# A two-branch linear-attention kernel on one core: x and V of the first two tiles by blocks of 128 rows, the first fold half a V later, the sums of K of tile 15 behind Q 12

## The chip, the core and the metric

The kernel runs on one core of a Trainium2 chip. A core has a matrix engine (TensorE, "PE" in the profile, with a separate row "PEld" for its weight loads), VectorE ("DVE"), ScalarE ("ACT"), GpSimd ("POOL") and SyncE ("SP"), which here issues nearly all DMAs. Each engine executes its own list of instructions in the order in which the program wrote it; semaphores hold an instruction back until what it reads has been written. The metric is device time in microseconds (us) of one execution, the median over runs.

## The reference

Two branches A and B of the same form read the same x and differ in weights only. S is 2048, D is 448, there are 16 heads of 28.

```python
qkv = (x @ wqkv).reshape(B, S, 3, H, Dh)            # q, k, v per head
pq  = einsum("bhsd,hdf->bhsf", q, w_phi)            # pk the same from k
phi_q = concat([softmax(pq), softmax(-pq)])         # over the 28 features; phi_k too
kv  = einsum("bhsf,bhsd->bhfd", phi_k, v);  z = phi_k.sum(s)
num = einsum("bhqf,bhfd->bhqd", phi_q, kv)
o   = num / (einsum("bhqf,bhf->bhq", phi_q, z) + 1e-6)
out_branch = o.reshape(B, S, D) @ wo
g   = sigmoid((x * gate_w).sum(-1))
result = g * out_A + (1 - g) * out_B
```

No position waits for an earlier one, but the sum kv over all 2048 positions has to be complete before the first num.

## The kernel before

The 2048 positions go in 16 tiles of 128. f32 accuracy comes from splitting each operand in a high part (written by ACT) and a low part (the rest, by a subtraction on DVE or POOL); one projection of a tile in one branch is 11 matmuls (4 high by high, 4 high by low, 3 low by high; the last 64 rows of x carry their low part in the same block). w_phi is multiplied into the weights of K and Q once, at the start: this is the fold. There are four folds F 0 to F 3, each one group of matmuls into the bank F, one transpose on DVE out of the bank (L363, into `ret` for F 0 and F 2, into `ru` for F 1 and F 3), high parts on ACT (`rk` for K, `rq` for Q) and low parts on DVE or POOL.

The stages, in the order of PE's program: 22 short warm-up records of matmuls on zeros (11 matmuls, L640, and 12 small ones, L643); V of tiles 0 and 1 (`v_first`, L448), in which the first block of x, the raw weights of V and their split arrive piece by piece; V of tiles 2 to 4 with the four folds between them; then for each tile K, Q and V projections (L416), the accumulation of kv (L501, name `T`), and at the end num (`N`, L583) and the output projection (`O`, L631) by pairs of tiles.

What follows K of a tile t (`k_soft`): ACT copies it to `pk`; DVE takes its maximum and minimum per head (`mx`, L482 and L483); POOL subtracts (`ret<-pk,mx` and `ret<-mx,pk`); ACT takes exp; DVE sums (`sm`, L489) and takes the reciprocal (L490); POOL multiplies (`ret<-ret,sm`). The two halves are called e. kv of two tiles needs their four multiplied halves. What follows Q (`q_front`, `q_soft`): DVE takes `qmx` (L516) out of the bank Q and writes `ru<-Q,qmx` twice, which frees the bank; four DMAs write that to `qd`, one reads it back; minimum `qmn` (L535), subtraction on POOL, exp, sums `qsm` (L541), multiplication and a transpose on DVE (L546). Of early tiles the result is spilled to DRAM and fetched back before num.

wo is rearranged in DRAM (`wos`, a row of copies from `in_wo`), and `split_wo` takes its seven blocks one after the other: load into `wst`, high part on ACT, low part on POOL (`wst<-wst`), and two stores to `wod`. One buffer serves all seven.

Who does what in which order is decided by the class `Plan`. Each step is added with engine, cost, latency and what it reads and writes; PE's steps stand in the order of the generator `steps()`. `order()` then simulates all engines and gives each free engine the ready step with the earliest due time; an extra `ahead` or `now` moves a step's due time, and a step with `two` set holds POOL and DVE apart from each other in that simulation. The result is a fixed list per engine. So a change in one place can move steps of another engine far away, because their turn is found anew.

```python
def split_wo(c):
    add("SP", 0.4, dma(s[0], wos[:, :, c]...), [...("wos", c)...], [("ws", 0)], lat=2.4, kb=229)
    put("ACT", D, act(f[1], s[0]), [("ws", 0)], [("ws", 1)])
    put("POOL", D, tt("POOL", f[2], s[0], s[1], OP.subtract), [("ws", 0), ("ws", 1)], [("ws", 2)])
```

## Time and profile before

| | before |
|---|---|
| median of 3 runs | 338.69 us (338.41 to 338.84) |
| the profiled execution | 338.63 us |
| its span in the trace | 336.8 us |
| PE busy | 330.2 us, 98% |
| DVE busy | 280.1 us, 83% |
| POOL busy | 251.0 us, 75% |
| ACT busy | 144.7 us, 43% |

The span runs from the first to the last instruction that the trace shows; 1.83 us of the profiled execution lie around it. A busy PE here means that PE had a matmul in flight: matmuls are pipelined, so their durations overlap, and the distance between the starts of two of them is what one costs. A row of the timeline gives start, duration, engine, line, operation, output and inputs, the count of merged neighbours, and in brackets how long the engine had been idle and what ended that. A weight load or matmul that starts late shows PE's waits; everything on the other engines counts only as far as it makes PE start late.

### The profile page before, as it was taken

To read this page: it belongs to the slowest core of one execution; us is meant where nothing else is said; L and a number is where in the kernel's file an instruction comes from. 1 tells how busy PE (TensorE), PEld (TensorE's weight loads), DVE (VectorE), ACT (ScalarE), POOL (GpSimd) and SP (SyncE) were. 2 spreads that over 40 slices of the span, in tenths; PEclk is the share of its full clock that TensorE was granted. 3 is DMA by queue.
4 is the path that set the end of the run, shared out by engine and by line. 5 is a ranking of instruction groups with operands and counts; after the bars stand their busy time and mean duration, and the time that the engine had idled before them with its cause. 6 is when DMAs were issued, how large, how long until landed. Compare 5 with 4: busy or idle time off the path is not lost.

```text
span 336.8 us, 8893 instructions
## 1 busy us (share of the span) xinstructions
PE 330.2 (98%) x3742; PEld 296.1 (88%) x3742; DVE 280.1 (83%) x339; ACT 144.7 (43%) x236; POOL 251.0 (75%) x210
## 2 busy tenths in 40 slices
PE   8999999999999999999999999989999999999995
PEld 7977899998999999999999999979788898788894
DVE  4547979798798795969999989985899999999960
ACT  4647845453264462624436244531052432533231
POOL 7118769999999879989896999982279768887400
PEclk9999999999999999999999999999999999999999
DMA  7882046532296847646556230875975455141011
GB/s 245 250 239 72 0 142 193 154 109 56 86 331 234 260 158 245 171 172 211 200 171 229 72 110 8 279 262 132 336 260 167 150 168 199 68 163 57 31 55 55
DMA packets 29855, 54.73 MB, mean 163 GB/s; under 512 B 4616, under 2 KB 25464, under 8 KB 27512
## 3 DMA queue, kind: packets, MB, share of 16 engines
q1 hardware_dynamic: 29560, 54.06, 49.5%
q8 instruction: 29, 0.48, 0.6%
q0 software_dynamic: 256, 0.12, 0.1%
q14 instruction: 10, 0.08, 0.1%
HBM read 31.54 MB, written 24.22 MB: 166 GB/s over the span
## 4 chain that ended last, share of the span: by engine, by line
DVE 33%; PE 30%; POOL 13%; DMA 12%; issue 5%; ACT 2%; SPq 2%; POOLq 0%; DVEq 0%; ACTq 0%
PE O L631 10%; POOL ret L263 8%; PE Q L416 5%; DMA qd<-ru 4%; DVE ret L546 4%; DVE sm L489 4%; DMA ru<-qd 4%; PE VB L416 3%; DVE qsm L541 3%; DVE ru L263 3%; DMA ed<-ret 3%; POOL rv L603 3%; DVE qmx L516 3%; PE VA L416 3%; DVE mx L482 3%
## 5 line engine op out<-in xcount | busy, mean ns | idle before, releaser
L416 PE MATMUL Q<-rq,rx 128*128 128x432 f32 x352 | 72.2, 359 | 1.3 <-DVE ru L263 1.2
L416 PE MATMUL K<-rk,rx 128*128 128x432 f32 x352 | 71.8, 359 | 0.0
L631 PE MATMUL O<-rk,rx 128*128 128x448 f32 x336 | 70.6, 368 | 0.1
L416 PEld LDWEIGHTS Q<-rq,rx 128*128 128x128 f32 x352 | 65.8, 188 | 5.4 <-DVE ru L263 2.0
L631 PEld LDWEIGHTS O<-rk,rx 128*128 128x128 f32 x336 | 62.5, 188 | 8.5 <-ACT rx L622 1.2
L416 PEld LDWEIGHTS K<-rk,rx 128*128 128x128 f32 x352 | 66.1, 188 | 3.1
L266 ACT ACTIVATE ret<-ret 128x896 f32<-128x896 f32 x48 | 45.6, 950 | 51.0 <-POOL ret L263 50.9
L263 POOL TENSOR_TENSOR ret<-ret,sm 128x896 f32<-128x896 f32 x32 | 54.0, 1707 | 3.4 <-DVE sm L490 3.3
L489 DVE TENSOR_REDUCE sm<-ret 128x32 f32<-128x896 f32 x32 | 33.7, 1070 | 4.7 <-ACT ret L266 4.7
L546 DVE STREAM_TRANSPOSE ret<-ret 128x2048 f32<-128x2048 f32 x16 | 36.5, 2283 | 1.1 <-POOL ret L263 0.8
L416 PE MATMUL VA<-rv,rx 128*128 128x450 f32 x154 | 34.3, 370 | 0.0
L541 DVE TENSOR_REDUCE qsm<-ret 128x32 f32<-128x896 f32 x32 | 33.2, 1056 | 1.3 <-ACT ret L266 1.1
L263 POOL TENSOR_TENSOR ret<-pk,mx 128x896 f32<-128x896 f32 x16 | 27.3, 1705 | 9.3 <-DVE mx L482 8.5
L416 PE MATMUL VB<-rv,rx 128*128 128x448 f32 x154 | 33.9, 367 | 0.0
L263 POOL TENSOR_TENSOR ret<-qmn,ru 128x896 f32<-128x896 f32 x16 | 28.2, 1764 | 7.1 <-DVE ret L546 4.2
L266 ACT ACTIVATE ret<-ru 128x896 f32<-128x896 f32 x16 | 15.2, 952 | 40.0 <-issue 17.4
L416 PEld LDWEIGHTS VB<-rv,rx 128*128 128x128 f32 x154 | 28.6, 188 | 3.4 <-issue 0.8
L416 PEld LDWEIGHTS VA<-rv,rx 128*128 128x128 f32 x154 | 28.7, 189 | 2.9 <-ACT rk L266 0.4
L263 POOL TENSOR_TENSOR ret<-ret,qsm 128x896 f32<-128x896 f32 x16 | 27.3, 1707 | 0.9
L263 POOL TENSOR_TENSOR ret<-mx,pk 128x896 f32<-128x896 f32 x16 | 27.3, 1706 | 0.7 <-DVE mx L483 0.7
L535 DVE TENSOR_REDUCE qmn<-ru 128x32 f32<-128x896 f32 x16 | 17.0, 1063 | 10.4 <-DMA ru<-qd 10.4
L603 POOL TENSOR_TENSOR rv<-rv,rd 128x896 f32<-128x896 f32 x14 | 23.8, 1703 | 1.1
(92 smaller groups left out, 444.3 us busy)
## 6 DMA issues: line engine op xcount, KB each, us to landing
ed<-ret SPq DMA_DIRECT2D x8, 1024.0 KB
ret<-ed SPq DMA_DIRECT2D x8, 1024.0 KB
qd<-ru SPq DMA_DIRECT2D x64, 112.0 KB
ru<-qd SPq DMA_DIRECT2D x16, 448.0 KB
out<-ret SPq DMA_DIRECT2D x16, 224.0 KB
wod<-wst SPq DMA_DIRECT2D x14, 224.0 KB
rk<-wod SPq DMA_DIRECT2D x2, 1568.0 KB
xraw<-in_xt SPq DMA_DIRECT2D x6, 512.0 KB
```

The lines of the kernel that those rows point to most:

```text
L263: return lambda: ENG[eng].tensor_tensor(val(o), val(a), val(b), op)
L266: return lambda: A.activation(val(o), val(i), f, **k)
L416: nc.tensor.matmul(bank[name][:, k, lo:hi], x[:, xc, o:o + P], w[l][:, c], start=i == 0, stop=i == len(XT) - 1)
L482: put("DVE", 2 * D, lambda: V.tensor_reduce(mh[0], pkh, AX.X, OP.max), kp, [km[0]])
L489: put("DVE", 2 * D, lambda s=s, e3=e3: V.tensor_reduce(sm[:, s], e3, AX.X, OP.add), [ke[s]], [("sm", t % 2, s)])
L516: put("DVE", 2 * D, lambda: V.tensor_reduce(mx, p4(), AX.X, OP.max), ["Q"], [km])
L535: put("DVE", 2 * D, lambda: V.tensor_reduce(qmn, tq.rearrange("p c b g f -> p c (b g) f"), AX.X, OP.min), [kt], [kn])
L541: put("DVE", 2 * D, lambda s=s, e3=e3: V.tensor_reduce(qsm[:, s], e3, AX.X, OP.add), [ke[s]], [("qsm", i, s)])
L546: add("DVE", 2.25, lambda: V.transpose(eTf[slot], eq.rearrange("p s a c f -> p (s a c f)")), ke, turned(slot))
L603: put(eng, 2 * D, lambda: ENG[eng].tensor_tensor(mid["o", n % 3].rearrange("p (c a f) -> p a c f", c=4, a=8), ctv()[:, :, i, :, :DH], rd[: ...
L631: nc.tensor.matmul(bank[pb][:, 0, :D], a, w, start=i == 0, stop=i == len(terms) - 1)
```

## The change

1. **Start.** x of tiles 0 and 1 is loaded in four DMAs of 128 rows (before: one of 128 rows and one of 384), alternating with the four loads of the raw weights of V for branch A. Its split goes by blocks: four ACT copies and four subtractions on DVE, and the one DVE copy of 384 rows (L297) is gone. V of tiles 0 and 1 takes its 11 pairs of matmuls block by block, and branch B takes both tiles in turns as branch A does. The warm-up has 9 and 14 matmuls in place of 11 and 12.
2. **Folds.** F 0 stands behind both halves of V 2 (before: between them); F 1 stays ahead of the second half of V 3. The raw loads for the folds go by another order of rows.
3. **K's sums of tile 15** are behind Q 12: the step `ks 15` is listed after it, its two sums carry a dependence on `ru` of Q 12, and the minimum and the sums of Q's tiles from 10 on carry one on the last sum of tile 15.

The first tables of the listing, and the parts of the diff that act on the engines' order:

```diff
-WARM, SMALL = 11, 12
+WARM, SMALL = 9, 14
 def steps():
-    yield from (("V01", 0, 0, 1), ("x1",), ("V01", 1, 0), ("V01", 1, 1), ("wt", 0), ("wt", 1), ("x", 2), ("wt", 2), ("wt", 3), ("V", 2, 0), ("F", 0, "DP"), ("V", 2, 1))
+    yield from (("V01", 0, 0, 1), ("x1",), ("V01", 1, 0, 1), ("wt", 0), ("wt", 1), ("x", 2), ("wt", 2), ("wt", 3), ("V", 2, 0), ("V", 2, 1), ("F", 0, "DP"))
...
-    yield from (("K", 14), ("V", 14, 0), ("k", 15, 0), ("k", 15, 1), ("kv", 12, 13), ("wo", 5), ("ks", 15), ("load_wo",), ("Q", 12), ("V", 14, 1), ("V", 15, 0), ("Q", 13))
+    yield from (("K", 14), ("V", 14, 0), ("k", 15, 0), ("k", 15, 1), ("kv", 12, 13), ("wo", 5), ("load_wo",), ("Q", 12), ("ks", 15), ("V", 14, 1), ("V", 15, 0), ("Q", 13))
...
 def load_x0():
-        for i, (lo, hi) in enumerate(((0, 1), (1, 4))):
-            if i:
-                load_wv(0, 0)
-            add("SP", 0.4, dma(xraw[:, lo:hi], ...), [], [("x0raw", i)], lat=3, kb=184 * (hi - lo), ahead=9000.0 - 2000 * i)
+        for c in range(4):
+            add("SP", 0.4, dma(xraw[:, c], xd[c * P:c * P + P, :2 * P]), [], [("x0raw", c)], lat=3 if c == 0 else 2, kb=131, ahead=9000.0 - 1000 * c)
+            load_wv(c, 0)
...
 def split_x0():
-        put("DVE", 6 * P, lambda: V.tensor_copy(t[:, 1:4], xraw[:, 1:]), [("x0raw", 1)], ...)
+        for c in range(4):
+            put("ACT", 2 * P, act(t[:, c], xraw[:, c]), [("x0raw", c)], [("x0h", c)])
+            if c < 3:
+                low_part("DVE", 2 * P, t[:, 4 + c], xraw[:, c], f[:, c], ...)
...
 def load_wt(n):
-        for q in (0, 2, 1, 3):
-            for k in range(2):
+        for j in range(8):
+            k, q = j % 2, (0, 1, 2, 3, 1, 0, 3, 2)[j]
...
 def v_first(b, ts):
-                 for c, i in ((0, 0), (0, 1), (1, 0), (0, 2), (1, 1), (2, 0), (1, 2), (2, 1), (3, 0), (2, 2), (3, 1))]
+                 for c, i in [(c, i) for c in range(4) for i in range(3) if (c, i) != (3, 2)]]
...
 def k_soft(t):
-            put("DVE", ..., V.tensor_reduce(sm[:, s], e3, AX.X, OP.add), [ke[s]], [("sm", t % 2, s)])
+            put("DVE", ..., V.tensor_reduce(sm[:, s], e3, AX.X, OP.add), [ke[s], *([("u", 0, 1)] if t == 15 else [])], [("sm", t % 2, s)])
...
 def q_soft(k, slot):
+        late = [("sm", 1, 1)] if k >= JIT else []
-        put("DVE", ..., V.tensor_reduce(qmn, ...), [kt], [kn])
+        put("DVE", ..., V.tensor_reduce(qmn, ...), [kt, *late], [kn])
-            put("DVE", ..., V.tensor_reduce(qsm[:, s], ...), [ke[s]], [("qsm", i, s)])
+            put("DVE", ..., V.tensor_reduce(qsm[:, s], ...), [ke[s], *late], [("qsm", i, s)])
```

Beside what the diff names, the engines' lists come out differently in other places. The first is POOL at the first K tiles (`pk0`, `mx0`, `sm0` belong to even tiles, `pk1`, `mx1`, `sm1` to odd ones; `wst` is the raw, high and low part of a block of wo). Before:

```order
30 L263 TENSOR_TENSOR ret_66<-ret_66,sm0_86 128x896
31 L263 TENSOR_TENSOR ret_66<-pk1_69,mx1_85 128x896
32 L263 TENSOR_TENSOR ret_66<-mx1_85,pk1_69 128x896
33 L263 TENSOR_TENSOR ret_66<-ret_66,sm0_86 128x896
34 L263 TENSOR_TENSOR ret_66<-ret_66,sm1_87 128x896 x2
35 L263 TENSOR_TENSOR ret_66<-pk0_68,mx0_84 128x896
```

And now:

```order
31 L263 TENSOR_TENSOR ret_66<-ret_66,sm0_86 128x896
32 L263 TENSOR_TENSOR ret_66<-pk1_69,mx1_85 128x896
33 L263 TENSOR_TENSOR wst_76<-wst_76 128x448
34 L263 TENSOR_TENSOR ret_66<-mx1_85,pk1_69 128x896
35 L263 TENSOR_TENSOR ret_66<-ret_66,sm0_86 128x896
36 L263 TENSOR_TENSOR ret_66<-ret_66,sm1_87 128x896 x2
```

The low part of wo's first block stands between the two subtractions of tile 1; before it stood some fifty rows further on. Behind it the list is the same up to that place. On ACT the high part of that block now stands ahead of the exp of tile 1's first half, where it stood right behind it.

The second is DVE from `ru` of Q 11 to the sums of tile 15 (`qmx0`, `qsm0`, `qmn0` belong to Q's even tiles, `mx0` and `sm0` to K's even tiles, 14 here; left out are the row of the other half of `mx1` and three reciprocals). Before:

```order
175 L263 TENSOR_TENSOR ru_67<-Q_560,qmx1_89 128x4x112 x2
176 L482 TENSOR_REDUCE mx0_84<-pk0_68 128x32
177 L483 TENSOR_REDUCE mx0_84<-pk0_68 128x32
178 L546 STREAM_TRANSPOSE ret_66<-ret_66 128x2048
179 L489 TENSOR_REDUCE sm0_86<-ret_66 128x32
181 L541 TENSOR_REDUCE qsm0_92<-ret_66 128x32
182 L489 TENSOR_REDUCE sm0_86<-ret_66 128x32
183 L482 TENSOR_REDUCE mx1_85<-pk1_69 128x32
186 L541 TENSOR_REDUCE qsm0_92<-ret_66 128x32
188 L535 TENSOR_REDUCE qmn1_91<-ru_67 128x32
189 L516 TENSOR_REDUCE qmx0_88<-Q_560 128x32
190 L263 TENSOR_TENSOR ru_67<-Q_560,qmx0_88 128x4x112 x2
```

And now:

```order
175 L263 TENSOR_TENSOR ru_67<-Q_564,qmx1_89 128x4x112 x2
176 L546 STREAM_TRANSPOSE ret_66<-ret_66 128x2048
177 L481 TENSOR_REDUCE mx0_84<-pk0_68 128x32
178 L482 TENSOR_REDUCE mx0_84<-pk0_68 128x32
179 L488 TENSOR_REDUCE sm0_86<-ret_66 128x32
180 L481 TENSOR_REDUCE mx1_85<-pk1_69 128x32
181 L482 TENSOR_REDUCE mx1_85<-pk1_69 128x32
182 L488 TENSOR_REDUCE sm0_86<-ret_66 128x32
183 L489 RECIPROCAL sm0_86<-sm0_86 128x32 x2
184 L515 TENSOR_REDUCE qmx0_88<-Q_564 128x32
185 L263 TENSOR_TENSOR ru_67<-Q_564,qmx0_88 128x4x112 x2
186 L488 TENSOR_REDUCE sm1_87<-ret_66 128x32 x2
```

Three passes of Q's tiles 10 and 11 (`qsm0` twice, `qmn1`) that stood ahead of `qmx0` of Q 12 stand behind the sums of tile 15 (`sm1`) now, and the transpose of tile 9 has gone ahead of the maxima of tile 14.

The third is DVE at the folds, where the lows of x of tile 4 (`rx<-xraw`) and of the folds (`rk`) stand between the four transposes. Before:

```order
18 L363 STREAM_TRANSPOSE ret_66<-F_106 128x2048
19 L263 TENSOR_TENSOR rk_62<-ret_66,rk_62 128x2x8x27 x2
20 L363 STREAM_TRANSPOSE ru_67<-F_106 128x2048
21 L263 TENSOR_TENSOR rx_65<-xraw_75,rx_65 64x128
22 L263 TENSOR_TENSOR rx_65<-xraw_75,rx_65 128x3x128
23 L363 STREAM_TRANSPOSE ret_66<-F_106 128x2048
24 L263 TENSOR_TENSOR rk_62<-ru_67,rk_62 128x2x8x27
25 L363 STREAM_TRANSPOSE ru_67<-F_106 128x2048
```

And now:

```order
18 L362 STREAM_TRANSPOSE ret_66<-F_106 128x2048
19 L263 TENSOR_TENSOR rx_65<-xraw_75,rx_65 64x128
20 L263 TENSOR_TENSOR rx_65<-xraw_75,rx_65 128x3x128
21 L263 TENSOR_TENSOR rk_62<-ret_66,rk_62 128x2x8x27
22 L362 STREAM_TRANSPOSE ru_67<-F_106 128x2048
23 L263 TENSOR_TENSOR rk_62<-ret_66,rk_62 128x2x8x27
24 L263 TENSOR_TENSOR rk_62<-ru_67,rk_62 128x2x8x27
25 L362 STREAM_TRANSPOSE ret_66<-F_106 128x2048
26 L362 STREAM_TRANSPOSE ru_67<-F_106 128x2048
```

Between the second and the third transpose there are two lows of the folds now, one of F 0's and the first of F 1's, where the lows of x stood; those have gone ahead of the second transpose, and nothing is left between the third and the fourth.

More of the change, by code (lines that the diff above doesn't have):

```diff
@@ L333, in load_wp @@
                 i = wphi[:, b, q].rearrange("(g d) f -> d g f", g=4)
-                add("POOL", 0.6, lambda q=q, b=b, i=i: G.dma_start(wp[32 * q:32 * q + DH, b], i), [], [("wp", q)], lat=3)
+                add("POOL", 0.6, lambda q=q, b=b, i=i: G.dma_start(wp[32 * q:32 * q + DH, b], i), [], [("wp", q)], lat=3, two=False)
         add("DVE", 0.15, lambda: V.memset(wpd, 0.0), [], [("wpd",)])
@@ L534, in q_soft @@
         put("ACT", 2 * D, act(eq[:, 0, :, :, :DH], tv, AF.Exp), [kt], [ke[0]])
-        put("DVE", 2 * D, lambda: V.tensor_reduce(qmn, tq.rearrange("p c b g f -> p c (b g) f"), AX.X, OP.min), [kt], [kn])
+        late = [("sm", 1, 1)] if k >= JIT else []
+        put("DVE", 2 * D, lambda: V.tensor_reduce(qmn, tq.rearrange("p c b g f -> p c (b g) f"), AX.X, OP.min), [kt, *late], [kn])
         put("POOL", 2 * D, tt("POOL", eq[:, 1, :, :, :DH], qmn.rearrange("p c a -> p a c")[:, :, :, None].to_broadcast([P, 8, 4, DH]), tv, OP.subtract),
@@ L540, in q_soft @@
             e3 = eq[:, s].rearrange("p a c f -> p (a c) f")[:, :, :DH]
-            put("DVE", 2 * D, lambda s=s, e3=e3: V.tensor_reduce(qsm[:, s], e3, AX.X, OP.add), [ke[s]], [("qsm", i, s)])
+            put("DVE", 2 * D, lambda s=s, e3=e3: V.tensor_reduce(qsm[:, s], e3, AX.X, OP.add), [ke[s], *late], [("qsm", i, s)])
             if s:
@@ L645, in first @@
     def first(eng, cost, fn, w):
-        add(eng, cost, fn, [], w)
+        add(eng, cost, fn, [], w, two=False)
     wt0, wt1 = ([("wt", k, n, q) for k in range(2) for n in ns for q in range(4)] for ns in ((0, 1), (2, 3)))
@@ L651, in hedgehog_mix @@
     load_x0()
-    for b in range(2):
-        for c in range(4):
-            if c + b:
-                load_wv(c, b)
+    for c in range(4):
+        load_wv(c, 1)
     split_x0()
@@ L738, in hedgehog_mix @@
                 split_x(1, i * P, i * P + P, ("DVE", "POOL")[i])
-            plan.hand_over([("x0raw", i) for i in range(2)], [("xraw",)])
+            plan.hand_over([("x0raw", i) for i in range(4)], [("xraw",)])
             plan.hand_over([("x0" + k, i) for k in "hl" for i in range(4) if (k, i) != ("l", 3)], [(k, 0, i) for k in ("x", "xl") for i in range(2)])
```

24 lines of the change are left out of this document (10 added, 14 removed).

## The prediction

> **What bounds the kernel now.** I read the page's first part, then PE's waits, then a table by stages.
>
> ```profile
> span 336.8 us, 8893 instructions
> PE 330.2 (98%) x3742; PEld 296.1 (88%) x3742; DVE 280.1 (83%) x339; ACT 144.7 (43%) x236; POOL 251.0 (75%) x210
> PE Q L416 <- DVE ru L263: 1.2, 1, 1.2
> 80.00:120.00 40.00, 40.00 (x321) 37.61 (x320) 32.98 (x38) 18.97 (x30) 36.44 (x28) 1.00 0.67 220
> ```
>
> PE sets the end: 330.2 of 336.8 us, and all 40 of 40 in a middle stretch. The change leaves PE's real matmuls as they are and takes out only warm-up, so it can move nothing but PE's idle time. There is little of that: the time ahead of the first real matmul, small gaps at the folds, and one wait of 1.2 us for DVE near 222. POOL in the middle has 36.44 of 40 (the fifth busy column), which matters below. Times are summed against the profiled execution, 338.63 us for a span of 336.8 (1.83 lie around it); it is 0.06 under the median of 338.69.
>
> **The start.**
>
> ```profile
> 1.06:5.28 4.22, 4.22 (x20) 1.00 0.80 227
> 5.28:5.77 0.49, 0.49 (x4) 1.00 1.02 301
> 1.06 4.78 PE L640 MATMUL VB<-zero 128*128 128x128 f32 x22 [1.06 <-DVE zero L649]
> 5.77 0.32 PE L643 MATMUL F<-zero 32*32 32x32 f32 x24
> 6.02 0.47 PE L448 MATMUL VA<-rv,rx 128*128 128x450 f32 x1
> 4.77 0.40 ACT L266 ACTIVATE rx<-xraw 128x256 fp32r<-128x256 f32 x1
> 13.91 0.88 DVE L263 TENSOR_TENSOR rx<-ret,rx 64x128 fp32r<-64x128 f32 x2 [1.17 <-ACT rx L266]
> 15.47 2.39 PE L416 MATMUL VA<-rv,rx 128*128 128x450 f32 x11
> ```
>
> The 11 warm-up matmuls are 22 records from 1.06 to 5.77, 0.214 apart. Nine are 18: they end at 1.06 + 18 x 0.214 = 4.91. The 24 small records took 6.02 - 5.77 = 0.25, so 28 take 0.29: the first real matmul can start at 5.20, as the first block of x is split at 4.77 + 0.40 = 5.17. That is 0.82 early. But V 2 needs x of tiles 2 and 3, whose lows are ready at 13.91 + 0.88 = 14.79, and nothing loads them earlier. So V 2 starts at 14.75 or so and not at 15.47: 0.7 is won (bounds 0, if the blocks come no earlier than PE wants them now, and the whole 0.82).
>
> **The folds give most of it back.**
>
> ```profile
> 17.79 1.50 PE L358 MATMUL F<-ret,wpd 28*32 28x256 f32 x64
> 19.32 2.32 DVE L363 STREAM_TRANSPOSE ret<-F 128x2048 f32<-128x2048 f32 x1 [4.53 <-PE F L358]
> 25.41 2.32 DVE L363 STREAM_TRANSPOSE ru<-F 128x2048 f32<-128x2048 f32 x1 [0.48 <-PE F L358]
> 28.27 1.73 ACT L266 ACTIVATE rk<-ru 128x432 fp32r<-128x432 f32 x2
> 29.67 2.32 DVE L363 STREAM_TRANSPOSE ret<-F 128x2048 f32<-128x2048 f32 x1 [1.03 <-issue]
> 31.91 1.21 DVE L263 TENSOR_TENSOR rk<-ru,rk 128x432 fp32r<-128x432 f32 x1
> 34.37 2.32 DVE L363 STREAM_TRANSPOSE ru<-F 128x2048 f32<-128x2048 f32 x1 [1.26 <-POOL rq L263]
> ```
>
> What follows on K's and Q's weights hangs on the last transpose, at 34.37. A transpose follows its fold by 19.32 - 17.79 = 1.53 and takes 2.32, and the next fold needs the bank it empties. One half of V costs 2.23 (the distance of two of them further on, 217.79 and 220.02, quoted below). Now: F 0 at 14.75 + 2 x 2.23 = 19.21, first transpose 20.75 to 23.07, F 1 at 23.1. On DVE come the lows of x (0.88) and one low of F 0, for which ACT first copies (half of 1.73, to 23.95); it ends at about 24.9. Second transpose 24.95 to 27.27 (before 25.41: 0.46 ahead). ACT's two copies of `rk<-ru` end at 27.3 + 1.73 = 29.03, and the low that waits for the second stands ahead of the third transpose now: 29.05 to 30.26 by the 1.21 of its row. Third transpose 30.26 to 32.58 (before 29.67: 0.6 behind), F 3 at 32.6, and the last transpose 1.53 later, at 34.15. Before, it waited for POOL's `rq`; POOL gets its input 0.9 earlier and is no longer last. So the 0.7 shrinks to **-0.2**; bounds -0.8 (nothing of the start is lost) and +0.6 (the third transpose's delay stays).
>
> **POOL's new place for wo's first block.** This is the largest term, and the change does not speak of it.
>
> ```profile
> 51.51 1.70 POOL L263 TENSOR_TENSOR ret<-pk,mx 128x896 f32<-128x896 f32 x1
> 53.90 1.70 POOL L263 TENSOR_TENSOR ret<-mx,pk 128x896 f32<-128x896 f32 x1 [0.69 <-DVE mx L483]
> 44.33 6.88 SPq L269 DMA_DIRECT2D wos<-in_wo  x9
> 51.26 0.58 SPq L269 DMA_DIRECT2D wst<-wos  x1
> 54.17 0.58 ACT L266 ACTIVATE wst<-wst 128x448 fp32r<-128x448 f32 x1
> L263 POOL TENSOR_TENSOR wst<-wst x7: 1153/1162/1177, 90.8 to 148.4; 128x448 fp32r<-128x448 f32 x7
> 53.90:78.42 24.52, 24.52 (x302) 22.69 (x300) 22.66 (x30) 12.36 (x19) 24.30 (x16) 1.00 0.43 127
> 71.77 6.69 POOL L263 TENSOR_TENSOR ret<-ret,sm 128x896 f32<-128x896 f32 x4
> 78.51 0.84 PEld L501 LDWEIGHTS T<-ret,vs 128*29 128x29 f32 x64 [0.24 <-POOL ret L263]
> ```
>
> `wst<-wst` stands between these two subtractions now; its first run was at 90.8. It needs ACT's high part, which ends at 54.17 + 0.58 = 54.75, because the block is loaded behind nine copies that SP issues from 44.33 on. So POOL stands idle from 53.21 to 54.8, works 1.16, and begins the second subtraction at 55.96 in place of 53.90: 2.06 late. Is there slack behind it? From 53.90 to 78.42 POOL is busy 24.30 of 24.52: none. The list is the same there, so the four multiplications of 71.77 end 2.06 later, and the last of them is what kv of tiles 2 and 3 waits for already (0.24 at 78.51). PE has nothing to do ahead of it. **+2.06**, on top of the shift of the folds. The 1.16 saved at 90.8 brings nothing: PE has no wait there (40 of 40 from 80 to 120). Bounds: +0.47 (the block raw in time, so that 1.16 replaces the 0.69 of idle time) and +2.5 (ACT's exp of the first half, now behind its `wst`, is late as well).
>
> **Q 13.**
>
> ```profile
> 208.27 1.09 DVE L263 TENSOR_TENSOR ru<-Q,qmx 128x448 f32<-128x448 f32 x2
> 211.26 2.30 DVE L546 STREAM_TRANSPOSE ret<-ret 128x2048 f32<-128x2048 f32 x1
> 216.77 1.08 DVE L482 TENSOR_REDUCE mx<-pk 128x32 f32<-128x896 f32 x1
> 219.73 0.96 ACT L266 ACTIVATE ret<-ret 128x896 f32<-128x896 f32 x1 [3.07 <-POOL ret L263]
> 222.40 1.16 DVE L263 TENSOR_TENSOR ru<-Q,qmx 128x448 f32<-128x448 f32 x2
> 225.46 0.56 DVE L490 RECIPROCAL sm<-sm 128x32 f32<-128x32 f32 x2
> 217.79 2.39 PE L416 MATMUL VB<-rv,rx 128*128 128x448 f32 x11
> 220.02 2.42 PE L416 MATMUL VA<-rv,rx 128*128 128x450 f32 x11
> 223.61 4.57 PE L416 MATMUL Q<-rq,rx 128*128 128x432 f32 x22 [1.17 <-DVE ru L263]
> 232.05 4.60 PE L416 MATMUL Q<-rq,rx 128*128 128x432 f32 x22
> 233.69 0.84 SPq L269 DMA_DIRECT2D ret<-ed  x2
> 233.69:243.77 10.08, 10.08 (x166) 8.34 (x164) 6.61 (x6) 0.00 (x0) 1.34 (x2) 1.00 0.89 297
> ```
>
> Q 13 could have started at 220.02 + 2.23 = 222.25, so the wait cost 1.36. By the new list from the same start: `ru` of Q 11 until 209.3, the transpose until 211.6, two maxima of tile 14 (1.08 each, which overlap by 0.1) until 213.6. POOL's subtractions (1.70 each) end at 214.3 and 216.0, the first exp at 215.3, its sum at 216.3; two maxima of tile 15 until 218.3, the other sum 219.4, reciprocals 219.9, `qmx` of Q 12 220.9, `ru` 222.1. If ACT takes the exp of Q 10 and a copy of `pk` ahead of the first exp, as its list has it, all this is 0.8 later, 222.9. In either case PE's own need has moved by the 1.86 lost above, to 224.1, and DVE has had time to catch up. **-1.36** (bounds -1.36 and -0.7, what is left where neither helps and ACT is late). The moved passes are hidden by PE's work up to Q 14: sums of tile 15 until 224.1, reciprocals 224.7, the three passes until 227.8, then `qmx` and `ru` of Q 13 until 230.2, and Q 14, which needs the bank that `ru` empties, comes at 232.05 - 1.36 = 230.7. Without the 1.86 on PE that cover is 0.5 thin.
>
> The loads of the spilled tiles (`ret<-ed`) do not get earlier with PE: ahead of them on SP stands the load of Q 12's `ru`, whose buffer POOL frees only with its subtraction of Q 10, now behind the last multiplication of tile 15. That I work out to 229.8 (reciprocals 224.7, two multiplications and the subtraction of 1.70), and with nine DMAs of 0.42 from there the loads are issued at 233.6 as before, while num of the second pair, which begins where this window ends, at 243.77, would come 1.36 sooner. Two loads of 1.05 MB at 297 GB/s take 7.1 and end at 240.8, ahead of 242.4: 0. If they ended just in time before, it costs 1.36. I take **+0.3**, nearer to the rate's answer.
>
> **Sum**: -0.2 + 2.06 - 1.36 + 0.3 = +0.8, so 338.63 + 0.8 = 339.4 us.
>
> **The rivals.**
>
> *Faster: wo's block is there in time.* SP's nine copies took 6.88, 0.76 each; other loads in this trace take SP 0.4 (the two `ret<-ed` 0.84). At 0.4 the load would be issued at 48, be split before 53.2, and POOL would lose 0.47 in place of 2.06. With no wait at num: -0.2 + 0.47 - 1.36 = -1.1, 337.5 us; with the 0.3, 337.8. I put it at 337.7. For it: all stages that hang on the folds come earlier if the start's gain survives. Against it: the copies are the same rows in the same order, and the price of 0.76 each is theirs.
>
> *Slower: a wait takes the place of Q 13's.* The fetch decides: if its transfers end at the same absolute time, as its unmoved issue says, num waits the full 1.36, and the removed wait is only moved by 20 us: 339.4 + 1.06 = 340.5. It decides as soon as the loads take over 8.7 us. For it: DMA is busy 0.89 there; against it: the rate above.
>
> *Slower: the rate of the first matmuls.* The records of the warm-up are 0.211 apart (20 in 4.22) until 5.28 and half that after it (4 in 0.49). If the doubled rate has to be earned by work that the change takes out, the real matmuls start at half rate; with one more stretch of 4.22, half of that is lost: 339.4 + 2.1, 341.5. Against it: PE is busy without a pause over 5.28 in both kernels, and by time alone the switch comes where it came, just behind the new first matmul. [...]
>
> *The change does not do what it says at the start.* That is in the forecast: a first matmul 0.8 earlier, and the last transpose where it was.
>
> **How the numbers follow.** The forecast has 0.55, with its own range of 338.8 to 340.2 (the folds' bounds); faster by an early block 0.22; the wait moved to num 0.15; the rate 0.05; 0.03 for what I don't see. About 0.2%, 0.7 us, is what a measurement of this kernel tells from no change: under 338.0 is faster, over 339.4 slower. The forecast lies on that edge and splits evenly, 0.27 and 0.28; the early block gives 0.20 faster and 0.02 same; num and the rate are slower. Together 0.21, 0.29 and 0.50. The range of 337.8 to 340.7 cuts off half of the early block and the rate.
>
> **What would show it.** The first matmul of `v_first` at 5.2 and the last fold transpose near 34.2 show the start given back. POOL's `wst` near 54.8 with an idle of 1.6 ahead of it, and a wait of PE at the second half of kv of tiles 2 and 3, about 2.1 + 0.2 long, show the main term; if PE has no such wait over 1, I am wrong there. The row "PE Q <- DVE ru" must be gone. A wait of PE for a DMA `ret<-ed` at num of the second pair shows the fourth term.

## The result, and the profile after

| | before | the change |
|---|---|---|
| median on one chip, 4 runs each | 338.76 us (338.41 to 339.13) | 343.75 us (342.88 to 344.32) |
| the profiled execution | 338.63 us | 343.85 us |
| its span | 336.8 us (336.76) | 342.0 us (342.04) |

The ratio is 1.0145, with a 95% interval of 1.012 to 1.0169: slower by about 5 us, or 1.5%. The forecast of 339.4 us had the side right and missed the size by 4.4; the time lies outside its range.

The difference is found by setting the starts of the same matmuls side by side in the two traces. The numbers are after minus before, in us; the third column is the part that the stretch from the row above adds. The last column is a second profile of the same changed program from another execution, against the same before.

| place | shift | added there | forecast | shift, second profile |
|---|---|---|---|---|
| first matmul of V 2 | -0.05 | -0.05 | -0.7 | 0.29 |
| first matmul of Q 0, behind the folds | 2.38 | 2.43 | 0.5 | 1.30 |
| behind kv of tiles 2 and 3 (Q 4) | 4.91 | 2.53 | 2.06 | 5.20 |
| Q 13 | 3.58 | -1.33 | -1.36 | 3.87 |
| last matmul | 3.71 | 0.13 | 0.3 | 4.70 |
| end of the span | 5.27 | 1.56 | 0 | 6.22 |

So the forecast's two largest prices were near; the folds were missed by 2.6 (start and folds together 2.38 against -0.2), and the end of the program was not in it.

**PE's waits.** The view of the waits by releaser, of the profile after (line and what it waited for, total, times, longest; the wait for `zero` at the start is in every profile, 1.06 long before):

```profile
PE T L500 <- POOL ret L263: 2.6, 2, 2.3
PE F L357 <- DVE ru L362: 1.5, 1, 1.5
PE VB L640 <- DVE zero L649: 1.1, 1, 1.1
PE F L357 <- DVE ret L362: 0.9, 1, 0.9
```

The row "PE Q <- DVE ru" of before is gone. In its place stand kv of tiles 2 and 3 (2.3 in one wait, of which 0.24 were there before) and two waits of the folds' matmuls.

**The start.** The timeline of after:

```profile
5.53 0.74 PE L447 MATMUL VA<-rv,rx 128*128 128x450 f32 x1
6.07 0.58 PE L447 MATMUL K<-rv,rx 128*128 128x450 f32 x1
6.45 0.43 PE L447 MATMUL VA<-rv,rx 128*128 128x450 f32 x1
7.07 0.54 SPq L269 DMA_DIRECT2D ret<-in_xt  x1
15.42 2.41 PE L415 MATMUL VA<-rv,rx 128*128 128x450 f32 x11
```

The first real matmul came 0.49 earlier (5.53, before 6.02), and V 2 began where it began. The 44 matmuls between them took 9.89 in place of 9.45: the first were 0.54 and 0.38 apart where the rest are some 0.21 apart, and small waits for the second block of raw weights stayed. The trace's records of the granted clock begin with full speed at 6.56 in this execution and at 5.41 in that of before; ahead of its first record the clock column of the views reads 1.00 for want of one. In the other profiles, too, the first distance was 0.44 or 0.54 where that record came 0.3 or more behind the first real matmul, and 0.31 to 0.34 where it came ahead of it or at most 0.09 behind. x of tiles 2 and 3 is loaded 1.34 later than before (5.73 there), behind twelve loads that SP issues one by one, where it stood behind ten.

**The folds.** ACT, VectorE, POOL, PE and VectorE again, in the timeline of after:

```profile
24.81 0.63 ACT L266 ACTIVATE rx<-xraw 128x512 fp32r<-128x512 f32 x1 [4.17 <-DMA xraw<-in_xt]
25.35 1.71 ACT L266 ACTIVATE rk<-ret 128x432 fp32r<-128x432 f32 x2
27.18 2.31 DVE L362 STREAM_TRANSPOSE ru<-F 128x2048 f32<-128x2048 f32 x1
27.90 1.33 POOL L263 TENSOR_TENSOR rq<-ret,rq 128x432 fp32r<-128x432 f32 x1 [5.32 <-ACT rq L266]
29.55 1.79 PE L357 MATMUL F<-ret,wpd 28*32 28x256 f32 x64 [1.45 <-DVE ru L362]
34.62 1.81 PE L357 MATMUL F<-ret,wpd 28*32 28x256 f32 x64 [0.85 <-DVE ret L362]
36.55 2.32 DVE L362 STREAM_TRANSPOSE ru<-F 128x2048 f32<-128x2048 f32 x1 [1.99 <-POOL rq L263]
```

The last transpose starts at 36.55 (before 34.37, forecast 34.15). Ahead of the first `rk` on ACT stands the split of x of tile 4, and it waits 4.17 for its load. At the end POOL's `rq` is last again, 0.12 behind PE's F 3 (34.62 + 1.81 = 36.43).

**wo's first block.** SP, ACT, POOL and PE:

```profile
53.95 0.59 SPq L269 DMA_DIRECT2D wst<-wos  x1
57.17 0.58 ACT L266 ACTIVATE wst<-wst 128x448 fp32r<-128x448 f32 x1 [2.45 <-DMA wst<-wos]
57.83 1.16 POOL L263 TENSOR_TENSOR wst<-wst 128x448 fp32r<-128x448 f32 x1 [2.25 <-ACT wst L266]
58.94 1.71 POOL L263 TENSOR_TENSOR ret<-mx,pk 128x896 f32<-128x896 f32 x1
83.44 0.99 PE L500 MATMUL T<-ret,vs 128*29 128x56 f32 x64 [2.32 <-POOL ret L263]
```

This is the chain that was forecast, with its second blocker visible: not POOL alone but ACT, too, waits for the block. (Counted in the trace, 24 operations of POOL stand between the block's place now and its place before, not some fifty.)

**Q 13, num and the end.** VectorE, PE, SP and ACT:

```profile
224.45 1.16 DVE L263 TENSOR_TENSOR ru<-Q,qmx 128x448 f32<-128x448 f32 x2
227.19 4.48 PE L415 MATMUL Q<-rq,rx 128*128 128x432 f32 x22
238.57 0.85 SPq L269 DMA_DIRECT2D ret<-ed  x2
336.74 0.54 ACT L266 ACTIVATE ret<-O 128x448 f32<-128x448 f32 x1 [3.73 <-PE O L631]
```

Q 13 has no wait. The last eviction of the output ends at 337.28, and the span at 342.04, 4.76 later; before it was 333.02 + 0.54 = 333.56 and 336.76, 3.20. What the DMA engines move in between is shown for before first, then for after (each from the end of the eviction to the end of the span, in 40 slices of 0.08 and 0.12 us; the share in tenths, and the rate):

```profile
DMA  0000000000389999972000000000000000000004
GB/s 0 0 0 0 0 0 0 0 0 0 133 332 354 398 398 420 465 266 67 0 0 0 0 0 0 0 0 0 0 0 0 0 0 0 0 0 0 0 0 101
```

```profile
DMA  0000000489993100000000000000000000000000
GB/s 0 0 0 0 0 0 0 197 349 425 364 364 122 69 0 0 30 15 15 15 30 15 0 0 0 0 0 0 0 0 0 0 0 0 0 0 0 0 0 0
q14 instruction: 1, 0.01, 0.4%
```

The last write of `out` is issued at the same distance, but in after a trickle of 15 to 30 GB/s follows it for 0.7 us, and a packet of the instruction queue, 8 KB, lies ahead of the trickle. The window of before has one such packet as well, but in its last slice, behind the write.

### The profile page after: what moved, and what is told of

Its sections match the earlier page's. It is cut to its first block, busy times and chain, and to the rows that moved or that the text cites. A ratio compares the mean times of both kernels' runs of the same rounds, so it can differ in the third digit from the quotient of the medians.

```text
span 342.0 us, 8902 instructions
## 1 busy us (share of the span) xinstructions
PE 330.5 (97%) x3742; PEld 296.7 (87%) x3742; DVE 280.7 (82%) x339; ACT 145.7 (43%) x239; POOL 251.3 (73%) x210
## 4 chain that ended last, share of the span: by engine, by line
PE 74%; DMA 9%; DVE 6%; SPq 5%; POOL 2%; issue 2%; ACT 0%; POOLq 0%; ACTq 0%
PE O L631 20%; PE Q L415 17%; PE K L415 14%; PE VA L415 7%; PE VB L415 7%; PE N L583 6%; SPq L269 5%; PE T L500 3%; DMA ret<-in_wkt 3%; DMA ret<-in_xt 2%; DMA xraw<-in_xt 1%; DVE sm L488 1%; POOL rq L263 1%; DVE rk L263 1%; DMA qd<-ru 1%
## 5 line engine op out<-in xcount | busy, mean ns | idle before, releaser
L263 POOL TENSOR_TENSOR ret<-ret,sm 128x896 f32<-128x896 f32 x32 | 53.9, 1705 | 2.8 <-DVE sm L489 2.7
L263 POOL TENSOR_TENSOR ret<-pk,mx 128x896 f32<-128x896 f32 x16 | 27.3, 1705 | 11.2 <-DVE mx L481 11.2
L263 POOL TENSOR_TENSOR ret<-qmn,ru 128x896 f32<-128x896 f32 x16 | 28.2, 1760 | 7.1 <-DVE ret L546 4.2
L263 POOL TENSOR_TENSOR ret<-ret,qsm 128x896 f32<-128x896 f32 x16 | 27.3, 1706 | 0.9
L263 POOL TENSOR_TENSOR ret<-mx,pk 128x896 f32<-128x896 f32 x16 | 27.3, 1706 | 0.0
L266 ACT ACTIVATE pk<-K 128x448 f32<-128x448 f32 x32 | 17.0, 537 | 18.9 <-PE K L415 17.4
```

Source lines behind the costliest of these rows:

```text
L263: return lambda: ENG[eng].tensor_tensor(val(o), val(a), val(b), op)
L266: return lambda: A.activation(val(o), val(i), f, **k)
```

## The experiments

The theory after the two traces had four parts: F 0, half a V later, starts a chain of transposes that does not get shorter; both pieces of wo's first block stand ahead of work that kv needs; part 3 wins what was forecast; the end is longer by something of its own. The rivals were that the start by blocks or the order of the raw loads are to blame for the folds, that POOL's piece of wo is the whole loss, and that part 3's gain comes back as another wait. The kernels are the change with a part undone, or the kernel before with one part alone. Each comparison is with before on the same chip.

### POOL's piece of wo back to its late place

```diff
-  put("POOL", D, tt("POOL", f[2], s[0], s[1], OP.subtract), [("ws", 0), ("ws", 1)], [("ws", 2)])
+  put("POOL", D, tt("POOL", f[2], s[0], s[1], OP.subtract), [("ws", 0), ("ws", 1), *([("qsm", 1, 1)] if c == 0 else [])], [("ws", 2)])
```

> The change, with one line more: the low part of wo's first block on POOL waits for the sums of Q 1 (a key in the planner only), so that it stands where it stood before. Theory POOL: its early place costs what PE waited at the second half of kv of tiles 2 and 3, 2.32 us in the profile of the change less the 0.24 that stood there before, and nothing else moves: 343.75 - 2.1 to 2.5 = 341.2 to 341.7, with no wait over 0.5 at that place. Rival: POOL was late by the folds' delay alone, which is still there, and the wait stays: 343.5 or more.

Measured: 342.09 us, ratio 1.0079 (1.0048 to 1.0111), between the ranges of the theory and the rival. kv of tiles 2 and 3 waits still, 1.85 in place of 2.32. ACT, VectorE, POOL and PE in that kernel:

```profile
56.49 0.58 ACT L266 ACTIVATE wst<-wst 128x448 fp32r<-128x448 f32 x1 [3.01 <-DMA wst<-wos]
56.97 0.94 ACT L266 ACTIVATE ret<-ret 128x896 f32<-128x896 f32 x1
57.94 1.09 DVE L488 TENSOR_REDUCE sm<-ret 128x32 f32<-128x896 f32 x1 [1.64 <-ACT ret L266]
59.56 1.71 POOL L263 TENSOR_TENSOR ret<-ret,sm 128x896 f32<-128x896 f32 x1 [1.20 <-DVE sm L489]
81.40 0.99 PE L500 MATMUL T<-ret,vs 128*29 128x56 f32 x64 [1.85 <-POOL ret L263]
```

POOL no longer stands still for the block, but ACT's high part does, with the exp of tile 1's first half behind it, then the sum, then POOL's multiplication. Between Q 0 and Q 4 this kernel loses 1.75 against before; the change loses 2.53. So ACT's piece alone is enough for most of the loss. POOL's piece alone was not run: it needs ACT's high part.

### Both pieces late

```diff
-  put("ACT", D, act(f[1], s[0]), [("ws", 0)], [("ws", 1)])
+  put("ACT", D, act(f[1], s[0]), [("ws", 0), *([("qsm", 1, 1)] if c == 0 else [])], [("ws", 1)])
```

beside the edit above.

> As the kernel in which POOL's low part of wo's first block stands late, and ACT's high part of it stands late as well (the same key). There ACT waited 3.01 us for that block ahead of the exp of tile 1's first half, and POOL's multiplications had 1.20 and 0.62 of idle time behind it. Theory: with both gone PE has no wait over 0.5 at kv of tiles 2 and 3, 1.75 less than with POOL's alone, 1.0 to 1.3 over the kernel before less the 1.36 of Q 13, so 339.0 to 339.6. Rival: POOL is late by the folds, and 1.5 or more of that wait stays: 341 or more.

Measured: 339.4 us, ratio 0.9992 (0.9963 to 1.0022), where the change itself, on the same chip, took 344.46. No wait of PE at kv is left; the waits of this kernel (the head of the view):

```profile
PE VB L640 <- DVE zero L649: 1.1, 1, 1.1
PE F L357 <- DVE ret L362: 0.9, 1, 0.9
PE F L357 <- DVE ru L362: 0.7, 1, 0.7
PE VA L447 <- ACT rv L266: 0.2, 1, 0.2
```

From Q 0 to Q 4 it loses nothing (1.94 and 1.93 against before). The 5 us between the two kernels are more than this stage's 2.5 to 3.9: the longer end of the span is gone as well here (4.20 behind the start of the last matmul, in the change 5.74), which the experiments on the end below take up.

### The change and before again, on that chip

> The change as it is, once more, beside the others of this set. In its first profile x of tile 4 arrived at 24.8 us and held ACT's copies of the first fold up; with the same lists but for wo's block it arrived at 22.6. Theory of the order: the last fold transpose is 1 us or more late whatever this load does, 35.3 to 36.6, and the time 1.0% to 1.7% over the kernel before. Theory of the loads: the transpose follows the load's arrival, and with 22.6 it is at 34.5.

> The kernel before as it is, for a profile beside this set: first real matmul 6.0 to 6.4, V of tile 2 at 15.5 to 15.8, last fold transpose at 34.4 to 34.7, wait of 1.2 to 1.4 ahead of Q 13.

The change took 344.46 us (ratio 1.0129, 1.0062 to 1.0196), before 338.97 over all its runs. In the second profile of before the rows lie where they were expected, but for the first real matmul, which came at 5.87. Both profiles are worth a look, since they are the same programs as the two above.

In the second profile of the change x of tile 4 came earlier (its split began at 23.39), F 2 did not wait, and the folds cost 1.01 from V 2 to Q 0 in place of 2.43. The last transpose began at 35.48, inside the range of the theory of the order. In exchange kv cost 3.90 from Q 0 to Q 4 in place of 2.53, although PE's wait was the same 2.32. The stage table of the second profile (columns: busy time and count of PE, PEld, DVE, ACT, POOL; granted clock, DMA share, GB/s), then of the first, for the stretch of kv's second half and what follows:

```profile
78.98:82.29 3.31, 0.99 (x64) 0.84 (x64) 3.27 (x5) 0.00 (x0) 3.31 (x3) 0.97 0.00 0
82.29:85.56 3.27, 3.27 (x68) 2.98 (x69) 1.57 (x3) 0.95 (x1) 3.27 (x3) 0.51 0.30 71
```

```profile
83.44:86.71 3.27, 3.27 (x76) 3.03 (x76) 1.74 (x3) 0.96 (x1) 3.27 (x3) 1.00 0.30 74
```

The granted clock was 0.51 over the 3.27 us behind the wait in one execution and 1.00 in the other, and 68 matmuls fit in where 76 did. From kv's second half to the second half of V it took 4.70 in place of 3.27, so the clock cost 1.4. PE's idle time ahead of it was 2.32 in both. What differs between the two traces is where the wait fell against the clock's records. In the second profile these stand at 6.97, 82.06, 85.47 and 341.48, all whole multiples of 3.413 apart, and 2.09 of the idle time (79.97 to 82.29) lie ahead of the one at 82.06, where the half clock begins (1.00 from 79 to 82, 0.52 from 82 to 84). In the first they stand at 6.56 and 341.07, 98 times 3.413 apart, and none lies near the wait; an estimate that counts 22 times 3.413 on from 6.56 comes to 81.66, which cuts the wait into 0.54 and 1.78. That this decided is a reading of two traces and not an experiment.

The second profile of before, 1.6 longer than the first, has a gap that the first has not (PE, output projection of the first pair, then the same place of the first profile):

```profile
246.97 1.48 PE L631 MATMUL O<-rk,rx 128*128 128x448 f32 x6
249.82 2.40 PE L631 MATMUL O<-rk,rx 128*128 128x448 f32 x11 [1.37 <-issue]
```

```profile
246.46 3.72 PE L631 MATMUL O<-rk,rx 128*128 128x448 f32 x16
```

The view names no releaser. Such gaps of 0.2 to 1.4 came at this place in eight of the sixteen profiles, of changed kernels and unchanged ones. The packets of the DMA engines divide the sixteen: at this place each trace has one packet of 16 KB of an instruction queue. In the eight profiles without a gap it began 0.85 to 1.37 ahead of the first matmul of this projection; in the eight with one it began between 0.76 ahead and 0.39 behind, and PE went on 1.2 to 1.5 behind its end (here it ran from 247.12 to 248.31, and PE went on at 249.82). That PE waited there for its next instructions is a reading of these times; no run moved this packet on purpose. A difference of under 1.5 between two single profiles has to be read from the stage that it lies in.

### Fold 0 back between the halves of V 2

```diff
-  ... ("V", 2, 0), ("V", 2, 1), ("F", 0, "DP"))
+  ... ("V", 2, 0), ("F", 0, "DP"), ("V", 2, 1))
```

> The change with the first fold back between the two halves of V 2. By the lists wo's first block and the lows on DVE then also stand where they stood before, so the start by blocks, the order of the raw loads and part 3 are left. Theory of the order (the folds' 2.4 us come from the first fold's later place and from the lows of x ahead of the folds' parts): 343.75 - 2.4 - 2.3 = 339.0, or 338.0 if the end of the last DMA, 1.5 later in the profile of the change, was chance. Theory of the loads (they come 1.2 us later because two more DMAs stand ahead of them): the last fold's raw weights still come late, 1.2 of the 2.4 stay, 340.2.

Measured: 340.16 us, ratio 1.0031 (1.0007 to 1.0056). With this one edit the planner puts both pieces of wo back where they stood, too, and kv waits 0.3. From V 2 to Q 0 the kernel loses nothing (0.74 and 0.68), with the start by blocks and the new order of the raw loads in it. So neither of these two is what the folds lost. What is left of 1.6 in the span lies in the end (5.72 behind the start of the last matmul); that the time meets the 340.2 of the theory of the loads is chance, since the folds lose nothing.

### Fold 0 behind V 2, alone

The same edit the other way round, in the kernel before.

> The kernel before with the first fold behind both halves of V 2 alone. Theory of the order: the first transpose comes 0.9 us later (one half V, 2.23, less the wait of 0.5 and the gaps behind), ACT and DVE wait for x of tile 4 ahead of the folds' parts, and the last transpose is 1 to 2 us late: 339.7 to 340.7. Theory of the loads: the order alone costs at most 0.3 us, 338.7 to 339.0, as the last transpose waited for POOL in the kernel before.

Measured: 340.44 us, ratio 1.0038 (1.0017 to 1.0058). From V 2 to Q 0 it loses 1.42 (0.28 and 1.70). PE's waits there (the rows of the folds and Q 0):

```profile
PE F L358 <- DVE ru L363: 0.7, 1, 0.7
PE Q L416 <- DVE Q L678: 0.4, 1, 0.4
```

So the place of F 0 costs 1.4 without the start and without the new order of raw loads. The split of x of tile 4 has gone ahead of the first `rk` by this edit, too, and its load was in time here (22.12, before the first transpose ended). The wo block has not moved: from Q 0 to Q 4 nothing is lost (0.08). It takes F 0's place and the rest of the change together to bring it forward. A second effect showed: Q 13 waits 1.8 here, not 1.2, and two kv stages ahead of it lose 0.7 together; what delays them was not traced. This profile is of a long execution, 341.77, so the 1.4 of the folds stands on its stage and on the median, 1.1 over before.

### x of tile 4 behind the first fold's copies

```diff
...
-    yield from (... ("V", 2, 0), ("V", 2, 1), ("F", 0, "DP"))
+    yield from (... ("V", 2, 0), ("V", 2, 1), ("F", 0, "DP"), ("xs",))
...
-            if a[0] == 2:
-                split_x(2, 0, P, "DVE")
...
+        elif what == "xs":
+            split_x(2, 0, P, "DVE", after=[("q", "h", 0, 0, 2)], late=("k", "l", 0, 0, 2))
...
```

> The change, with one thing moved: the split of x of tile 4 (ACT's rx<-xraw 128x512 and VectorE's two low parts) stands behind rk and rq of fold 0 and behind the second F transpose, as it does before the change, instead of ahead of the first rk. In the profile of the change that rx waited 4.17 us for its load, until 24.81, with rk of fold 0 behind it (25.35); in its second profile the load came at 23.39 and rk began at 24.20, 0.34 behind the end of the transpose. Theory A (what the folds lost is x of tile 4 at the head of ACT's and VectorE's queues): rk begins at the end of the first transpose (about 23.9 to 24.2), the wait of the third fold (1.45) goes, V of tile 4's second half begins 1.0 to 1.5 earlier than in the change, 342.2 to 342.8. Theory B (it is fold 0 itself, half a V of 2.38 later, and the chain of transposes behind it): the last fold and V 4b move by less than 0.4, 343.3 to 344.3.

Measured: 344.6 us, ratio 1.016 (1.0102 to 1.0218). The expectation's first step came true in part (`rk` began at 24.55, in the change at 25.35), and its sum did not. VectorE and PE:

```profile
26.35 2.31 DVE L362 STREAM_TRANSPOSE ru<-F 128x2048 f32<-128x2048 f32 x1
28.72 1.79 PE L357 MATMUL F<-ret,wpd 28*32 28x256 f32 x64 [0.47 <-DVE ru L362]
29.58 2.99 DVE L263 TENSOR_TENSOR rx<-xraw,rx 64x128 fp32r<-64x128 f32 x2
33.51 2.31 DVE L362 STREAM_TRANSPOSE ret<-F 128x2048 f32<-128x2048 f32 x1
35.87 1.79 PE L357 MATMUL F<-ret,wpd 28*32 28x256 f32 x64 [2.35 <-DVE ret L362]
```

The wait of F 2 fell from 1.45 to 0.47, and that of F 3 rose from 0.85 to 2.35: the two lows of x now stand between the second and the third transpose, and they took 2.99 there, where they took 0.86 ahead of the second. POOL works on its own lows at that time (2.04 from 28.73 and 1.44 from 30.71). So both theories fall in part: x is one cost of the chain, but neither of the two places tried for it is free (waits of 1.45 and 0.85 in the one, of 0.47 and 2.35 in the other).

### Part 3 alone

```diff
-  ... ("wo", 5), ("ks", 15), ("load_wo",), ("Q", 12), ...
+  ... ("wo", 5), ("load_wo",), ("Q", 12), ("ks", 15), ...
```

with the two dependences of part 3, in the kernel before.

> The kernel before with part 3 alone (K's sums of tile 15 behind Q 12). Main: the wait of 1.36 us ahead of Q 13 goes, and num of the second pair waits 0.3 to 0.5 for the fetched tile, as in the profile of the change (0.47 over two gaps): 338.7 - 1.36 + 0.4 = 337.7. Rival: the fetch ends at the same absolute time as before and the wait is only moved: 338.5 to 338.8, with 1.3 at num. Second rival: DVE is late without the lead that the stall of the change gave it, and Q 13 still waits 0.6: 338.3.

> The kernel before with part 3 alone (K's sums of tile 15 behind Q 12 on VectorE) once more, for its interval against before: the wait of 1.36 at Q 13 is gone and num and fetch give 0.2 to 0.5 back, so 0.9 to 1.4 less than before if nothing else moves: ratio 0.9960 to 0.9975. If the first measurement (0.9965) was of that chip alone, 0.998 to 1.0.

> The kernel before with part 3 alone, on the same chip as the variant beside it: 0.9 to 1.4 below before (0.996 to 0.9975), and by account A at or below the other variant.

Measured on three chips: 337.73 us (ratio 0.9965, 0.9949 to 0.9982), 338.84 (0.9977, 0.9947 to 1.0007) and 338.34 (0.9988, 0.9966 to 1.001). In all three profiles the wait at Q 13 is gone, and Q 14 does not wait either; this is the whole view of PE's waits in the third:

```profile
PE VB L641 <- DVE zero L650: 1.1, 1, 1.1
```

From Q 4 to Q 13 the shift changes by -1.33, -1.33 and -1.33, to the last matmul by +0.05, +1.02 and -0.07 more. So 0.3 to 1.4 is kept. All three medians lie under those of before, but only the first of the three intervals lies wholly under 1; it is the fastest kernel of this study. The second profile was long for other reasons: V of tiles 0 and 1 waited 1.4 and 0.5 for raw weights in that execution, the output projection had its gap of 0.7, and num waited 0.5 for `ret<-ed`. That last one is the wait at num that was named as a rival, at half its price and in one profile of three.

### The start alone

The change with its folds, its order of raw loads and part 3 undone: blocks of x, V of tiles 0 and 1 block by block, the shorter warm-up.

> The kernel before with the start alone (blocks of x and V of tiles 0 and 1, shorter warm-up). The folds, POOL's list and the tail stand as before. Theory now: the second block of V's raw weights arrives no earlier than before (6.7 to 7.4 in the profiles with blocks, 6.3 to 6.6 in those without), PE waits 0.7 to 1.3 for it, and V of tile 2 begins at 15.4 to 16.2 as before: 338.7 to 339.4, no gain. The forecast's theory: V of tile 2 begins 0.7 us earlier, at 14.75, and 0 to 0.7 of it reaches the end: 338.0 to 338.7.

Measured: 341.18 us, ratio 1.0064 (1.003 to 1.0098). This is over the ranges of both theories. V 2 begins 0.24 later than before, so the start wins nothing. Most of the span's 3.7 comes from elsewhere:

```profile
PE Q L415 <- DVE ru L263: 1.5, 1, 1.5
PE T L500 <- POOL ret L263: 1.4, 1, 1.4
PE VB L639 <- DVE zero L648: 1.1, 1, 1.1
PE O L630 <- issue: 0.9, 1, 0.9
PE VA L447 <- ACT rv L266: 0.5, 1, 0.5
```

kv of tiles 2 and 3 costs 1.27 (Q 0 to Q 4), behind a `ru` of Q that was read back 1.35 later than in the second profile of before (ACT's exp begins at 65.60 there, 64.25 in the other). The gap at the output projection has 0.9, and the end 1.31.

### The end of the span

In sixteen profiles the end of the span lies either 4.17 to 4.60 or 5.49 to 5.74 behind the start of the last matmul. The packets of the trace divide them without exception. In the six long ones a packet of the instruction queue begins 2.02 to 2.60 behind that start, while the write of the last rows is in flight (from 1.85 on), and the write's last packet begins at 3.40 to 3.56. In the ten short ones no such packet lies between 1.85 and 2.57, and the write's last one begins at 2.56 or 2.57. The delay sits in one sixteenth of the write: 135 of its 144 packets have begun by 2.57 in all sixteen, and in the six the other nine begin where the instruction packet ends (2.91 in after, 2.60 + 0.31) and follow one another. To move that packet, some writes of `out` were issued in halves:

```diff
-        add("SP", 0.4, dma(out[t * P:(t + 1) * P, :], obs[n % 2]), [("ob", n % 2)], [], lat=2.2, kb=229)
+        for lo, hi in ((0, 64), (64, P)) if n in (2, 3, 4, 5) else ((0, P),):
+            add("SP", 0.4, dma(out[t * P + lo:t * P + hi, :], obs[n % 2][lo:hi]), [("ob", n % 2)], [], lat=2.2, kb=229 * (hi - lo) // P)
```

> The change, in which the writes of out of four tiles (the third to the sixth) are issued in two halves each: the same bytes, four more DMA instructions on SP, everything else row for row as in the change. Theory A (an instruction fetch of SP lies amid the last write): the fetch comes some writes earlier, as in the variant with both of wo's pieces late (14.3 us ahead), the span ends 4.2 instead of 5.7 behind the last matmul's start, and the time is 1.2 to 1.6 below the change, 342.2 to 342.8. Theory B (another engine's fetch, or another cause): 5.7 as in the change, 343.4 to 344.4.

Measured: 342.65 us (ratio to before 1.0078, 1.0049 to 1.0106; the change has 1.0145). The packet moved from 2.60 behind that start to 2.91 ahead of it, and the span ends 4.38 behind the start of the last matmul. The two rows of the DMA engines, from 336.3, the end of the eviction, to the end of the span:

```profile
DMA  0000000000599999930000000000000000000003
GB/s 0 0 0 0 0 0 0 0 0 0 232 443 401 379 379 401 359 106 0 0 0 0 0 0 0 0 0 0 0 0 0 0 0 0 0 0 0 0 0 96
```

The trickle is gone. The other direction, two writes halved in the kernel before (`n in (2, 3)` in the same line):

> The kernel before, in which the writes of out of the third and the fourth tile are issued in two halves each (64 rows): the same bytes, two more DMA instructions on SP at a place where SP is idle, everything else row for row as before. In five of six profiles of kernels that start by blocks a packet of the instruction queue of 8 KB lies 2.0 to 2.6 us behind the last matmul's start, amid the last write of out, and the write's last packet ends at 3.4 to 3.6 instead of 2.57; the span ends 5.5 to 5.75 behind that matmul instead of 4.2. Theory A (the start by blocks has two more DMA instructions on SP, which shift that fetch into the last write): here too the span ends about 5.6 behind the last matmul's start, and the kernel takes 1.2 to 1.6 more than before, 340.2 to 340.8 if before is 339.0. Theory B (the fetch belongs to another engine, or the longer end has another cause): the end stays at 4.2, and the time is that of before within 0.3.

Measured: 339.39 us, ratio 1.0 (0.9969 to 1.0031). The end stayed in the short group (4.60); the packet lay at 4.54, where it had been at 4.16, behind the write in both. So the cause of the long end is shown (four more instructions on SP, and the packet, the trickle and 1.4 us go), but not how many instructions bring it in: two, which the start by blocks adds on SP, were not enough here. The late packets are 0.8 to 1.0 of it; another half a microsecond lies between the write's last packet and the end of the span (2.2 in after, 1.6 before), and no row explains it.

### Fold 0 back, and the packet out of the last write

Both edits together leave the start by blocks, the order of the raw loads and part 3.

> The change with fold 0 back between the halves of V 2 and with the writes of out of four tiles in two halves each, as in the variant before: what is left of the change is the start by blocks, the order of the raw loads and part 3. Account A (fold 0's place costs the folds and both pieces of wo, 3.5 to 5 together, and the instruction fetch in the last write 1.35): the sum is the kernel before less the wait at Q 13 (1.3) plus what num and fetch give back (0.2 to 0.5) plus nothing to 0.8 from the start: ratio 0.997 to 1.000 to before, the span ending 4.2 to 4.4 behind the last matmul's start. Account B (the start by blocks or the raw loads' order cost by themselves, as the 2.2 of the start alone seemed to say): above 1.003.

Measured: 338.78 us, ratio 1.0003 (0.9979 to 1.0027); part 3 alone, beside it, 338.34. The interval fits the first account and excludes the second. The span ends 4.38 behind the start of the last matmul, which itself is 0.23 earlier than before. kv of tiles 2 and 3 loses 1.13, as in the start alone, and part 3 wins 1.33. So the start and the order cost no more than that 1.1, and it is not in every execution: without the halved writes, the same lists lost 0.22 there.

## Why the prediction was wrong

**The start: wrong.** It let the first real matmul begin at 5.2 and V 2 at 14.75. The first came at 5.53 and V 2 at 15.42. Two steps failed. The 18 records of the warm-up ended at 5.20 and not at 4.91: the first distance is 0.37, and the average of 0.214 had taken in two shorter distances near the end of the 22 (0.18 and 0.11, where the rest behind the first are 0.21). And "V 2 needs x of tiles 2 and 3, ... and nothing loads them earlier" was not the bound: V 2 began 0.14 before their lows were ready (14.68 + 0.88 = 15.56, late as their load was). V of tiles 0 and 1 itself got longer, by 0.44, and took back what had been won. The third rival, the rate, was there in small: the first three records are 0.54, 0.38 and 0.26 apart, some 0.55 over the later distance; it had been priced at 2.1. What was said against it, that by time alone the switch comes where it came, does not hold: the first record of the full clock lies between 4.75 and 7.20 in the sixteen profiles. Where it came early, PE waited for the second block of raw weights instead (0.5 in the start alone), and over the nine profiles with the start by blocks V 2 began from 0.05 earlier to 0.74 later. That is the forecast's own bound of 0, "if the blocks come no earlier than PE wants them now".

**The folds: wrong, and the largest miss.** -0.2 was forecast, 2.38 measured (1.30 in the second profile), and the bound was +0.6. Three steps of the sum failed. Its chain began at 14.75, and the absent gain of the start made the first transpose 0.77 late (21.52 for 20.75). It let VectorE come to the lows of x straight behind the first transpose, but x of tile 4 came at 24.81 in one execution and at 23.39 in the other; the forecast had asked when the queue got there, and not when the data did. By the second transpose that had cost another 1.46 (27.18 for 24.95), in the second profile nothing. And the last transpose came 1.93 behind F 3's start, not 1.53: F 3 takes 1.81, where the 1.50 of F 0 had been used, and POOL ends 0.12 behind it. "POOL gets its input 0.9 earlier and is no longer last" is wrong: `rk` from the second transpose began at 29.52, before at 28.27, and POOL's first `rq` at 27.90, before at 24.74. The input came half a V later with F 0, 2.2 and more, and the slack in POOL's list, 1.48 before, could take up only part of it. The kernel with F 0's move alone gives the plain size: 1.4. That x is not the whole cause was shown by moving it, which only moved the wait from F 2 to F 3.

**wo's first block: right.** +2.06 was forecast and 2.53 measured, next to the upper bound of +2.5, and for that bound's reason: ACT's exp was late as well. A wait of 2.1 + 0.2 at kv was named and is 2.32. POOL's idle time ahead of the block was 2.25 and not 1.6, since the load came 0.3 later than the shift alone. What the forecast did not have is the 1.4 that the second profile lost behind this wait, at a granted clock of 0.51.

**Q 13: right.** -1.36 forecast, -1.33 measured, and in each kernel with part 3 alone again. VectorE was in time: `ru` of Q 12 ended at 225.6 (224.45 + 1.16), PE wanted it at 227.19. The 1.86 on PE that the forecast leaned on was not needed: with part 3 alone nothing is lost ahead, and the same 1.33 is won.

**num and the fetch: near in size, by luck in part.** +0.3 forecast, 0.13 measured; no wait for `ret<-ed` at num in the profile after, which was the sign that had been named. The loads did stay where they were, as forecast: they were issued 4.88 later than before (238.57 for 233.69), which is the shift ahead of Q 13. The 0.3 was a choice between two values, and other small gaps lie in the same stretch.

**The end: not in the sum.** 1.56 of the 5.27. The forecast took the span's end to follow the last matmul at a fixed distance. It came 4.17 to 5.74 behind that matmul's start in the sixteen profiles.

**The rivals.** "wo's block is there in time" fell: the nine copies took SP 7.21 in place of 6.88. "The wait moved to num" fell in the change; with part 3 alone it came once in three profiles, at 0.5. A rival that the profile of before could have given, and that was not on the list: the chain behind F 0 is as long as the V work that covers it, as its rows "[1.26 <-POOL rq L263]" and the small gaps at the folds said, so F 0 half a V later is a loss of most of that half, less what slack there is (1.42 of 2.23 with F 0's move alone).

## What to carry to other kernels

When a producer is moved behind a block of work, count from its new end through every queue of the chain, and check for each input that a queue meets when its data lands: a step that reaches the head of an in-order engine ahead of its data charges the wait to all that stands behind it (here ACT's split of x of tile 4 waited 4.17 for its load, and `rk` of F 0 behind it began at 25.35). A rearranged list can bring a harmless step (here one block of wo) ahead of its load on two engines at once, and putting one of them back repairs little (kv waited 1.85 in place of 2.32). And before a small change is judged by one profile, look at the stage in which the difference lies: here gaps of up to 1.4 came and went between executions of one program.
